# The last block's column halves copied out of PSUM by one VectorE instruction each, in place of a VectorE and a ScalarE copy

## Chip, cores, metric

The kernel runs on one core of one Trainium2 chip. The metric is device time of one execution in microseconds (us), lower is better. The kernel before takes 317.51 us (median of 3 runs, 317.42 to 317.64). Runs that agree are expected to lie within a few tenths of a per cent; a verdict of "faster" or "slower" is given only beyond 2%. A run is said to be fast when it is not over 1.5% above the fastest run of its kernel.

## The reference

Linear attention over 8 batches and 8 heads, then a gated feed-forward block. Cut to what matters:

```python
q_s = softmax(q, axis=-1);  k_s = softmax(k, axis=2)        # 8 x 8 x 576 x 64
kv  = einsum('bhsd,bhse->bhde', k_s, v)
x   = einsum('bhsd,bhde->bhse', q_s, kv)   # -> 4608 tokens x 512
g   = x @ w_gate;  val = x @ w_val         # 512 -> 1536
out = (silu(g) * val) @ w_out              # 1536 -> 512, float32
```

The change touches the last 128 tokens of the last product, the out-projection. Its matmuls write to a memory called PSUM, which is divided into banks; the result is copied from there to a second memory, SBUF (this copy is also called the evacuation), and the stores to the output read SBUF. A store is issued by an engine on its queue, and has landed when the semaphore that tells of its completion is updated.

## The kernel before

The out-projection is done in 36 blocks of 128 tokens. An ordinary block is 12 matmuls of 512 columns into one PSUM bank, one copy to SBUF, and two stores of 64 rows each, both on the sync queue:

```python
def o_out(j, o_ps, eng=nc.vector):
    o_sb = osb.tile([128, 512], FP32, tag="o_sb", name="o_sb")
    copy(eng, o_sb, o_ps)
    store(j, o_sb)                      # two stores, both on the sync queue
```

The last block is different, since nothing follows that could hide its copy and its stores. It is made in two column halves of 256, so that the first half is copied and stored while the second is multiplied, and each half's copy is shared between two engines:

```python
def o_last(j):
    r0 = (j * 128) % RING
    o_sb = osb.tile([128, 512], FP32, tag="o_sb", name="o_sb")
    for c0 in (0, 256):
        o_ps = bank("o_ps")                       # one PSUM bank per half
        for m in range(MT):                       # 12 matmuls of 256 columns
            nc.tensor.matmul(
                out=o_ps[:, 0:256], lhsT=hr[:, m, r0:r0 + 128], rhs=wo[:, m, c0:c0 + 256],
                start=(m == 0), stop=(m == MT - 1),
            )
        nc.vector.tensor_copy(out=o_sb[:, c0:c0 + 128], in_=o_ps[:, 0:128])
        nc.scalar.copy(out=o_sb[:, c0 + 128:c0 + 256], in_=o_ps[:, 128:256])
        store(j, o_sb, c0, c0 + 256, (nc.sync, nc.scalar))   # rows 0-63 sync, 64-127 scalar queue
```

A tile framework puts in the semaphores between engines.

The softmax here doesn't subtract the row's maximum and nothing guards it: scores larger than these inputs give would overflow.

## Time and profile before

| | before |
|---|---|
| time, median of 3 | 317.51 us |
| span of the profiled run | 316.0 us |
| matmul engine busy | 304.7 us, 96% |
| last matmul's end to the last stores' issue | 0.65 us |
| last stores' issue to landing (sync, scalar queue) | 1.93, 2.19 us |
| last matmul's end to the end of the span | 4.04 us |

(The last three rows are differences of time stamps in the trace.)

The page of the kernel before, its line of the span, its busy line and the head of the chain that ended last. PE is the matmul engine, DVE is VectorE, ACT is ScalarE:

```profile
span 316.0 us, 4856 instructions
PE 304.7 (96%) x1865; PEld 152.0 (48%) x1894; DVE 163.2 (52%) x277; ACT 147.6 (47%) x218; POOL 28.0 (9%) x35
PE 88%; DMA 4%; DVE 3%; ACT 2%; issue 1%; POOL 1%; SPq 0%; DVEq 0%
```

The kernel is bound by matmuls almost from end to end. The change can only act where no matmul hides anything, which is after the last one. The chain of waits there, of the kernel before (start, duration, what):

```profile
309.31 2.63 PE o_ps L342 x24
311.95 0.02 issue
311.97 0.30 DVE o_sb L346
312.27 0.02 issue
312.30 0.27 ACT o_sb L347
```

The same stretch in the timeline of the kernel before (start, duration, engine, line, operation; the bracket holds the engine's idle time before it and what ended it; SPq and ACTq are the issues of stores on the sync and the scalar queue):

```profile
311.97 0.29 DVE L346 COPY o_sb<-o_ps 128x128 f32<-128x128 f32 x1 [1.02 <-PE o_ps L342]
312.30 0.27 ACT L347 COPY o_sb<-o_ps 128x128 f32<-128x128 f32 x1 [1.04 <-DVE o_sb L346]
312.59 0.47 SPq L316 DMA_DIRECT2D out_dram<-o_sb  x1
312.59 0.50 ACTq L316 DMA_DIRECT2D out_dram<-o_sb  x1
```

The matmuls end at 311.94. ScalarE has been idle for a microsecond, and yet it starts its copy only when VectorE's ends. The view of waits of the last microseconds of the kernel before names it as well:

```profile
ACT o_sb L347 <- DVE o_sb L346: 1.0, 1, 1.0
DVE o_sb L346 <- PE o_ps L342: 1.0, 1, 1.0
```

So the sharing makes two copies in a row, not two at once. What VectorE copies from PSUM cost at several widths, from the groups of instructions by shape of the kernel before (count | busy us, mean ns | idle before):

```profile
L113 DVE COPY o_sb<-o_ps 128x512 f32<-128x512 f32 x33 | 22.4, 680 | 39.2 <-PE o_ps L322 37.3 <-remote 1.9
L113 DVE CAST xt<-xp 128x256 bf16<-128x256 f32 x5 | 2.0, 417 | 0.0
L346 DVE COPY o_sb<-o_ps 128x128 f32<-128x128 f32 x2 | 0.6, 292 | 1.6 <-PE o_ps L342 1.6
```

The mean of 680 ns for 512 columns mixes slightly different records; the copies of the last blocks, read one by one, take 691 to 692 ns.

### The profile page before, as it was taken

Reading aid. Unit: us, or ns where it says so; the run is one execution under the profiler, and the core shown is the slowest. Engines: PE = TensorE matmul, PEld = TensorE weight load, DVE = VectorE, ACT = ScalarE, POOL = GpSimd, SP = SyncE. Lnnn points to the kernel's source line nnn. Section 1 sums busy time; section 2 is a strip of 40 time slices with the busy share of each in tenths; the row PEclk is TensorE's granted clock in tenths of the full one; section 3 lists DMA queues with packets and bytes.
Section 4 is the critical chain, followed back from the end, with each engine's and each line's share of the span. In section 5 each row is a group of like instructions: output and inputs, shape, how many; then the busy total and the mean of one; then the engine's idle time right before and its main releaser. Section 6 shows DMA issues by size and latency. Waiting matters only on the chain.

```text
span 316.0 us, 4856 instructions
## 1 busy us (share of the span) xinstructions
PE 304.7 (96%) x1865; PEld 152.0 (48%) x1894; DVE 163.2 (52%) x277; ACT 147.6 (47%) x218; POOL 28.0 (9%) x35
## 2 busy tenths in 40 slices
PE   6799999999999999999999999999999999999994
PEld 2477744554444444544454444544454444444443
DVE  3834476685754566455835492639354333423421
ACT  4743488634663465447354637355743113312300
POOL 2930021100200020002000200020000000000000
PEclk9999999999999999999999999999999999999999
DMA  7999999269246806490629253944310202020124
GB/s 269 183 204 207 296 393 391 68 160 364 50 91 179 338 17 128 112 394 11 141 68 352 97 110 66 322 162 103 66 41 0 65 3 66 0 68 3 31 68 102
DMA packets 39304, 45.75 MB, mean 145 GB/s; under 512 B 16368, under 2 KB 23024, under 8 KB 39280
## 3 DMA queue, kind: packets, MB, share of 16 engines
q1 hardware_dynamic: 32480, 39.99, 42.0%
q0 software_dynamic: 6640, 5.31, 10.9%
q8 instruction: 15, 0.25, 0.3%
q10 hardware_dynamic: 160, 0.13, 0.2%
q14 instruction: 9, 0.07, 0.1%
HBM read 37.75 MB, written 9.44 MB: 149 GB/s over the span
## 4 chain that ended last, share of the span: by engine, by line
PE 88%; DMA 4%; DVE 3%; ACT 2%; issue 1%; POOL 1%; SPq 0%; DVEq 0%
PE g_ps L298 29%; PE u_ps L298 29%; PE o_ps L322 25%; PE kv L191 3%; DMA wv<-in_moe_w_val_dram 2%; DMA k<-in_k_dram 2%; DVE rs L138 1%; PE xp L267 1%; DVE qs L152 1%; PE o_ps L342 1%; ACT L124 1%; ACT eq L124 1%; POOL v L361 0%; PE tp L166 0%; POOL v L358 0%
## 5 line engine op out<-in xcount | busy, mean ns | idle before, releaser
L305 ACT ACTIVATE sg<-g_ps 128x512 bf16<-128x512 f32 (+2 forms) x120 | 65.1, 554 | 139.1 <-PE g_ps L298 120.7
L306 DVE TENSOR_TENSOR hr<-sg,u_ps 128x512 bf16<-128x512 bf16 (+2 forms) x120 | 74.5, 630 | 87.8 <-PE u_ps L298 80.4
L298 PE MATMUL g_ps<-xt,wg 128*128 128x512 bf16 (+2 forms) x469 | 110.0, 358 | 1.0 <-ACT xt L111 0.2
L298 PE MATMUL u_ps<-xt,wv 128*128 128x512 bf16 (+2 forms) x468 | 109.8, 357 | 1.2 <-DMA wv<-in_moe_w_val_dram 0.5
L322 PE MATMUL o_ps<-wo,hr 128*128 128x512 bf16 x414 | 93.0, 379 | 0.4 <-issue 0.2
L298 PEld LDWEIGHTS <-wv 128*128 128x128 bf16 x480 | 46.9, 98 | 47.2 <-DMA wv<-in_moe_w_val_dram 0.9
L298 PEld LDWEIGHTS <-wg 128*128 128x128 bf16 x480 | 45.8, 98 | 45.3 <-issue 0.7
L322 PEld LDWEIGHTS <-hr 128*128 128x128 bf16 x420 | 40.9, 98 | 49.1
L113 DVE COPY o_sb<-o_ps 128x512 f32<-128x512 f32 x33 | 22.4, 680 | 39.2 <-PE o_ps L322 37.3
L127 POOL CAST vb<-v 128x1152 bf16<-128x1152 f32 x14 | 16.0, 1146 | 174.3 <-DMA v<-in_v_dram 111.8
L138 DVE TENSOR_REDUCE rs<-eq 128x18 f32<-128x1152 bf16 (+2 forms) x18 | 21.7, 1214 | 13.2 <-ACT eq L124 13.2
L152 DVE TENSOR_TENSOR qs<-eq,rr 128x1152 bf16<-128x1152 bf16 (+2 forms) x18 | 22.1, 1237 | 0.1
L124 ACT ACTIVATE eq<-q 128x1152 bf16<-128x1152 f32 (+2 forms) x18 | 18.1, 1050 | 4.5 <-DMA q<-in_q_dram 4.4
L124 ACT ACTIVATE ek<-k 128x1152 bf16<-128x1152 f32 x16 | 18.0, 1158 | 0.3 <-DMA k<-in_k_dram 0.2
L305 ACT ACT_TABLE_LOAD x12 | 15.4, 1283 | 0.2
L124 ACT ACT_TABLE_LOAD x11 | 14.1, 1283 | 0.2
L388 PE MATMUL idle<-zero 128*128 128x512 bf16 x20 | 6.1, 459 | 3.0 <-DVE rs L138 1.8
L191 PE MATMUL kv<-vb,ek 64*128 64x129 bf16 x252 | 8.7, 217 | 0.0
L191 PEld LDWEIGHTS <-ek 64*128 64x128 bf16 x252 | 7.3, 94 | 2.7 <-ACT sg L305 2.1
L275 ACT CAST xt<-xp 128x512 bf16<-128x512 f32 x12 | 6.4, 588 | 3.6 <-PE xp L267 3.6
L276 DVE CAST xt<-xp 128x512 bf16<-128x512 f32 x12 | 7.7, 683 | 0.0
L347 ACT COPY o_sb<-o_ps 128x128 f32<-128x128 f32 x2 | 0.5, 265 | 13.3 <-DVE o_sb L346 13.3
(46 smaller groups left out, 70.2 us busy)
## 6 DMA issues: line engine op xcount, KB each, us to landing
q<-in_q_dram SPq DMA_DIRECT2D x16, 576.0 KB, 5.6
k<-in_k_dram SPq DMA_DIRECT2D x16, 576.0 KB, 7.3
out_dram<-o_sb SPq DMA_DIRECT2D x70, 128.0 KB, 2.3
v<-in_v_dram SPq DMA_DIRECT2D x14, 576.0 KB, 9.0
wo<-in_moe_w_out_dram POOLq DMA_DIRECT2D x4, 384.0 KB, 16.3
wg<-in_moe_w_gate_dram POOLq DMA_DIRECT2D x2, 384.0 KB, 9.7
wv<-in_moe_w_val_dram POOLq DMA_DIRECT2D x2, 384.0 KB, 10.7
wg<-in_moe_w_gate_dram POOLq DMA_DIRECT2D x1, 512.0 KB, 13.7
```

What stands on the lines that cost most here:

```text
L113: eng.tensor_copy(out=out, in_=in_)
L124: nc.scalar.activation(out=e[:, t0:t1], in_=src[:, t0:t1], func=AF.Exp)
L127: nc.gpsimd.tensor_copy(out=vbs[G][:, :, 0:128].rearrange("p t (h d) -> p t h d", d=64), in_=raw["v", b, G].rearrange("p h (t d) -> p t h ...
L138: i = nc.vector.reduce_sum(out=rs[:, 2 * t0:2 * t1], in_=eq2[:, 2 * t0:2 * t1, :], axis=mybir.AxisListType.X)
L152: eng.tensor_mul(qs[:, t0:t1, :].rearrange("p t (h d) -> p (t h) d", d=64), eq2[:, 2 * t0:2 * t1, :], s["rr"][:, 2 * t0:2 * t1].to_broadca ...
L191: nc.tensor.matmul(out=kv[g][:, c:c + 129], lhsT=ek_of(b, G, g, t), rhs=vbs[G][r, t, 0:129], start=(t == 0), stop=(t == T - 1),)
L275: nc.scalar.copy(out=xt[:, 2 * G, c0:c0 + 512], in_=main[G][0])
L276: nc.vector.tensor_copy(out=xt[:, 2 * G + 1, c0:c0 + 512], in_=main[G][1])
L298: nc.tensor.matmul(out=gu[a][i][:, 0:w_], lhsT=(wg, wv)[a][:, kk, ms], rhs=xt[:, kk, c:c + w_], start=(kk == 0), stop=(kk == KT - 1),)
L305: nc.scalar.activation(out=sg[:, 0:w_], in_=g_ps[:, 0:w_], func=AF.Silu)
L306: nc.vector.tensor_mul(hr[:, m, r:r + w_], sg[:, 0:w_], u_ps[:, 0:w_])
L322: nc.tensor.matmul(out=o_ps, lhsT=hr[:, m, r0:r0 + 128], rhs=wo[:, m, :], start=(m == 0), stop=(m == MT - 1),)
```

## The change

The intent is to pay one copy's fixed cost and no hand-over between engines, in place of two fixed costs and a hand-over.

```diff
-            nc.vector.tensor_copy(out=o_sb[:, c0:c0 + 128], in_=o_ps[:, 0:128])
-            nc.scalar.copy(out=o_sb[:, c0 + 128:c0 + 256], in_=o_ps[:, 128:256])
+            nc.vector.tensor_copy(out=o_sb[:, c0:c0 + 256], in_=o_ps[:, 0:256])
             store(j, o_sb, c0, c0 + 256, (nc.sync, nc.scalar))
```

## The prediction

> **What bounds the kernel now.** The page of the profile before (span 316.0 us) has the matmul engine busy 96% of the span at a granted clock of 0.998; the chain of waits is 88% matmul. The change touches none of that, only the tail after the last matmul, where everything is exposed. The timeline of the last microseconds: last matmul of the second column half ends at 311.94 (chain of waits); VectorE copy 128x128 starts 311.97, takes 0.29; ScalarE copy 128x128 starts 312.30, takes 0.27; both store issues (sync and scalar queues) start at 312.59, take 0.5, land 1.9 and 2.2 us later; then closing waits, to 316.0. So the two copies do not run side by side: the view of waits says the ScalarE copy waited for the VectorE copy, though their columns are disjoint, and the built program has that wait. Both read one PSUM bank; the Trainium skill, "PSUM — Partial Sum Buffer", Terms, says no two engines may access the same bank at once. The trace agrees: 312.30 is after 312.26. No overlap is lost by giving up ScalarE.
>
> **What it removes and adds.** Per half it removes a ScalarE copy (265 ns) and one hand-over between engines (some 35 ns from end to start), and makes the VectorE copy 256 columns wide. VectorE took 692 ns for 128x512 f32 from PSUM and 292 ns for 128x128: 1.04 ns a column and about 159 ns fixed. An estimate from these for 128x256 is 425 ns (casts of 128x256 from PSUM took 417). The Trainium skill, "VectorE: DVE Perf Modes", errata section, gives 120 + columns cycles at 0.96 GHz for PSUM to SBUF, 392 ns for 256; the trace is 33 ns above that at both measured sizes, which again gives 425. Stores keep queues, sizes and order; in the built program they wait for VectorE in place of ScalarE. Everything earlier is unchanged.
>
> **On the critical path.** Matmul end to store issue is 0.65 us before (0.03 + 0.29 + 0.04 + 0.27 + 0.02). After: 0.03 + 0.425 + 0.02 = 0.47. Saved: 0.17 to 0.18 us, once. The first half gains the same, but its copies and stores lie under the second half's matmuls, so that is worth nothing.
>
> **Predicted time:** 317.51 - 0.17 = 317.34 us, 0.05% less. The spread of the three runs before (317.42 to 317.64) is larger than the gain, so medians may stand in either order; 8 times in 10 between 317.10 and 317.62. Chances: faster by over 2% 0.002, within 2% 0.996, slower by over 2% 0.002.
>
> **What would show each step right or wrong.** Right: one VectorE copy of 128x256 per half, 0.41 to 0.44 us; no ScalarE copy of the output block in the tail; both last stores issued 0.45 to 0.49 us after the last matmul; issue to landing (1.9 to 2.4 us) and landing to end unchanged; span near 315.8. Wrong: a copy over 0.55 us; stores that wait longer after the copy's end than now (0.02 us), above all on the scalar queue, which now waits for another engine instead of its own copy; a longer landing that gives the 0.17 us back.
>
> **What would make it wrong.** A copy cost not linear between the measured widths; a slower start of the scalar queue's store when that engine has been idle; landing times, which vary by 0.5 us among the last stores, hiding the gain in single runs.

## The result, and the profile after

The changed kernel takes 317.37 us (median of 6 runs, 317.25 to 318.02); the kernel before, in the same rounds and the earlier ones, 317.47 us (6 runs, 317.37 to 318.08). The ratio is 0.9998 with a 95% interval of 0.9985 to 1.0011. (Ratios here are the mean time of one kernel's fast runs over that of the other's of the same rounds, so they are not quite the ratios of the medians quoted.) At this resolution not even the sign is known: the interval is some 0.8 us wide, the expected gain is 0.17 us. What the change does has to be read from the trace.

The page of the kernel after, the same lines:

```profile
span 316.2 us, 4851 instructions
PE 306.3 (97%) x1865; PEld 152.5 (48%) x1894; DVE 163.3 (52%) x277; ACT 147.1 (47%) x216; POOL 28.1 (9%) x35
```

ScalarE has two instructions fewer and VectorE as many as before. The span of this run is 0.2 us longer, not shorter; it is the slowest of the six (318.02 us). Its chain of waits at the end:

```profile
309.48 2.63 PE o_ps L342 x24
312.11 0.02 issue
312.14 0.42 DVE o_sb L346
```

Its timeline after the last matmul:

```profile
312.14 0.42 DVE L346 COPY o_sb<-o_ps 128x256 f32<-128x256 f32 x1 [0.89 <-PE o_ps L342]
312.59 0.47 SPq L316 DMA_DIRECT2D out_dram<-o_sb  x1
312.60 0.50 ACTq L316 DMA_DIRECT2D out_dram<-o_sb  x1
```

And its line on the two copies, with their shortest, median and longest duration in ns:

```profile
L346 DVE COPY o_sb<-o_ps x2: 423/424/425, 310.8 to 312.1; 128x256 f32<-128x256 f32 x2
```

Three things are to be seen. The copy of 256 columns takes 424 ns, as predicted (425). From the last matmul's end to the issue of the last stores it is now 0.49 us, where it was 0.65: 0.16 us saved, as predicted within 0.02. And the last matmul itself ends 0.16 us later than in the profile before (312.10 against 311.94), although nothing before it was changed. Over the profiles of kernels that do the same work up to there (before, after, and the repeats below), this end lies between 311.46 and 312.11. That scatter of 0.65 us is four times the saving, and it is large enough to hide it in the medians.

There is one loose end. The stores of this profile land later after their issue than those of the profile before. The line on the landing of the last two stores (shortest, median, longest), first of before, then of after:

```profile
DMA to landing us min/median/max: 1.9/2.1/2.2
```

```profile
DMA to landing us min/median/max: 2.2/2.3/2.4
```

With the later landing, the time from the last matmul's end to the end of the span is 4.11 us after, against 4.04 before. If that is caused by the change, the saving is given back; if it is scatter, it is not. This was the first thing to test.

### The profile page after: what moved, and what is told of

Its sections match the earlier page's. It is cut to its first block, busy times and chain, and to the rows that moved or that the text cites. A ratio compares the mean times of both kernels' runs of the same rounds, so it can differ in the third digit from the quotient of the medians.

```text
span 316.2 us, 4851 instructions
## 1 busy us (share of the span) xinstructions
PE 306.3 (97%) x1865; PEld 152.5 (48%) x1894; DVE 163.3 (52%) x277; ACT 147.1 (47%) x216; POOL 28.1 (9%) x35
## 4 chain that ended last, share of the span: by engine, by line
PE 88%; DMA 4%; DVE 3%; ACT 2%; issue 1%; POOL 1%; SPq 0%; DVEq 0%
PE g_ps L298 29%; PE u_ps L298 29%; PE o_ps L322 25%; PE kv L191 3%; DMA wv<-in_moe_w_val_dram 2%; DMA k<-in_k_dram 2%; DVE rs L138 1%; PE xp L267 1%; DVE qs L152 1%; PE o_ps L342 1%; ACT L124 1%; ACT eq L124 1%; POOL v L360 0%; PE tp L166 0%; POOL v L357 0%
## 5 line engine op out<-in xcount | busy, mean ns | idle before, releaser
L387 PE MATMUL idle<-zero 128*128 128x512 bf16 x20 | 7.8, 555 | 2.7 <-DVE rs L138 1.5
L113 DVE CAST xt<-xp 128x128 bf16<-128x128 f32 (+2 forms) x14 | 4.9, 374 | 2.8 <-PE xp L220 2.8
```

What stands on the lines that cost most here:

```text
L113: eng.tensor_copy(out=out, in_=in_)
L387: i = nc.tensor.matmul(out=idle, lhsT=zero[:, 0:128], rhs=zero, start=True, stop=True)
```

## The experiments

Twelve kernels ran, all correct. The names used for theories are those of the expectations: A is that the saving is real, is the difference of one and two instructions in a row, and is kept; B is that slower landing gives it back.

### The changed kernel twice more, and the kernel before once more

No edit.

> The changed kernel once more, unaltered. Theory A (the saving of about 0.18 us before the last store issue is kept): last matmul to store issue 0.45 to 0.49 us again, issue to landing scattered between 1.9 and 2.4 us as before, time 0.1 to 0.25 us under the kernel before where the rounds can resolve it. Rival B (the saving is given back: landing became slower because of the change): both last stores land 2.2 to 2.4 us after issue again, 0.2 us more than the 1.9 and 2.2 of before, and the times are equal within 0.1 us.

> The kernel before once more, unaltered, for a second profile of it. Theory A: last matmul to store issue 0.64 to 0.66 us; issue to landing anywhere in 1.9 to 2.4 us, so that it may exceed that of the changed kernel. Rival B (landing is slower in the changed kernel because of the change): 1.9 and 2.2 us again. Time ratio 1.000 within 0.002.

> The changed kernel a third time. Last matmul to store issue 0.45 to 0.50 us; the scalar store lands 2.18 to 2.45 us after issue (2.40 and 2.21 in its two traces, 2.19 and 2.18 in those of before); if the saving is kept on the whole, last matmul to the end of the span is 3.87 to 3.95 us in most traces against 4.04 in both of before; if landing is slower because of the change, it is 4.05 or more again.

Measured, from the traces (us; the first row of each kernel is the profile shown above):

| profile | last matmul's end | to store issue | scalar store, issue to landing | sync store, issue to landing | last matmul's end to end of span |
|---|---|---|---|---|---|
| before | 311.94 | 0.65 | 2.19 | 1.93 | 4.04 |
| before, again | 311.46 | 0.65 | 2.18 | 1.92 | 4.04 |
| after | 312.10 | 0.49 | 2.40 | 2.21 | 4.11 |
| after, again | 312.11 | 0.49 | 2.21 | 1.92 | 3.91 |
| after, third | 311.67 | 0.49 | 2.20 | 1.92 | 3.89 |

The landing line of the third profile of after:

```profile
DMA to landing us min/median/max: 1.9/2.1/2.2
```

The longer landing did not come back, so B falls as a steady effect; that a late landing now and then is likelier after the change, three profiles against two cannot exclude. In two of three profiles the tail is 0.13 to 0.15 us shorter than before; the first profile had a landing 0.2 us late. In that profile the last data packets of the last stores ended 2.34 us after the last matmul, as in the other two (2.34 and 2.35) and earlier than before (2.50 and 2.49), so as far as the packet records go it was mainly the notice of completion that came late. Why it did is open.

The times again resolve nothing. After, again: 317.65 us against 317.56, ratio 0.9997 (0.9985 to 1.0010). After, third: 317.42 against 317.52, ratio 1.0005 (0.9991 to 1.0018). Before, again: 317.57 against 317.70, ratio 0.9995 (0.9980 to 1.0010); that is the kernel before compared with itself, and its ratio lies as far from 1 as the changed kernel's.

Pooled, the changed kernel has a mean of 317.53 us (16 runs, standard error 0.09) and the kernel before 317.58 us (35 runs, standard error 0.04): a difference of 0.05 with an error of 0.10, which fits nothing saved, and is also only a little over one error away from 0.17 us saved.

### The saving magnified 25 times

A gain too small for the clock can be repeated until it is large. In these kernels the second half's matmuls are done into two banks with the same values, and the evacuation is made 25 times over. The three differ only in who copies, and from which bank:

```diff
+            if c0 == 256:
+                o_p2 = bank("o_ps")
             for m in range(MT):
-                nc.tensor.matmul(out=o_ps[:, 0:256], ...)
+                for o in (o_p2, o_ps) if c0 == 256 else (o_ps,):
+                    nc.tensor.matmul(out=o[:, 0:256], ...)
+            for _ in range(25 if c0 == 256 else 1):
# many_one:
+                nc.vector.tensor_copy(out=o_sb[:, c0:c0 + 256], in_=o_ps[:, 0:256])
# many_split:
+                nc.vector.tensor_copy(out=o_sb[:, c0:c0 + 128], in_=o_ps[:, 0:128])
+                nc.scalar.copy(out=o_sb[:, c0 + 128:c0 + 256], in_=o_ps[:, 128:256])
# many_split_banks: as many_split, but
+                nc.scalar.copy(..., in_=(o_p2 if c0 else o_ps)[:, 128:256])
```

> The saving magnified. In the last half the matmuls are done into two banks (12 more of 256 columns, some 1.3 us), and the evacuation is made 25 times over (the same values): here one VectorE copy of 256 columns each time. Theory A: each repeat costs the 0.424 us of one copy plus 0.0 to 0.06 us of waiting for itself, 24 repeats add 10.2 to 11.6 us; total 328.8 to 330.3.

> As many_one, but each of the 25 evacuations is the pair of before, 128 columns on VectorE, then 128 on ScalarE, from one bank. Theory A (serial, two fixed costs and two hand-overs): 0.29 + 0.04 + 0.265 + 0.04 = 0.63 us a pair, 24 repeats add 15.1 us, total about 333.7, 3.5 to 5 us more than many_one (0.17 to 0.2 us each). A rival in which the pair's cost in the tail was a chance of one trace: no difference from many_one, or a shorter time.

> As many_split, same copies and sizes, same output tile, but ScalarE reads the second bank, with the same values. Theory A (only the shared bank makes the pair serial): the two engines run side by side, 0.29 to 0.36 us a pair, 24 repeats add 7 to 8.6 us, total 325.5 to 327.5, clearly under many_one. Rival E (the shared output tile, or the hand-over between the engines, makes the pair serial): still some 0.63 us a pair, total as many_split, about 333.7.

| | time (median of 4) | against before (317.70) | per evacuation, against one VectorE copy |
|---|---|---|---|
| one VectorE copy | 329.52 us | 1.0370 | |
| pair, one bank | 333.84 us | 1.0507 | +0.17 us (4.32 / 25) |
| pair, two banks | 326.29 us | 1.0269 | -0.13 us (-3.23 / 25) |

All three lie where theory A put them. The timelines, each of a stretch within the repeats; first one VectorE copy at a time (five copies in 2.26 us; a new one starts every 0.46 us, which is 0.424 of copy and 0.035 of waiting for itself):

```profile
315.62 2.26 DVE L350 COPY o_sb<-o_ps 128x256 f32<-128x256 f32 x5
```

The pair from one bank, where the engines take turns, a pair every 0.63 us:

```profile
315.72 0.29 DVE L350 COPY o_sb<-o_ps 128x128 f32<-128x128 f32 x1 [0.33 <-ACT o_sb L351]
316.05 0.27 ACT L351 COPY o_sb<-o_ps 128x128 f32<-128x128 f32 x1 [0.36 <-DVE o_sb L350]
316.34 0.29 DVE L350 COPY o_sb<-o_ps 128x128 f32<-128x128 f32 x1 [0.33 <-ACT o_sb L351]
```

The pair from two banks, where they run side by side, six in 1.92 us:

```profile
315.74 1.92 DVE L350 COPY o_sb<-o_ps 128x128 f32<-128x128 f32 x6
315.99 1.76 ACT L351 COPY o_sb<-o_ps 128x128 f32<-128x128 f32 x6
```

Two things follow. The 0.17 us per evacuation is shown on the clock, not only in the trace, and it passes in full into the time: the traces have 4.16 us between the ends of the last copies of the two, counted from the last matmul, and the times differ by 4.32. The tail hides nothing of it. And the reason why the split is slower is the shared bank: same engines, same sizes, same output tile, another bank, and the pair is the fastest of the three. Rival E falls. The two-bank form is no better kernel as it stands, for it computes the half twice; filling two banks without that means 24 matmuls of 128 columns in place of 12 of 256, which no run here tried.

### ScalarE alone for the last half

If the number of instructions in a row is what counts, the engine does not have to be VectorE.

```diff
-            nc.vector.tensor_copy(out=o_sb[:, c0:c0 + 256], in_=o_ps[:, 0:256])
+            if c0 == 0:
+                nc.vector.tensor_copy(out=o_sb[:, c0:c0 + 256], in_=o_ps[:, 0:256])
+            else:
+                nc.scalar.copy(out=o_sb[:, c0:c0 + 256], in_=o_ps[:, 0:256])
```

> The last half copied by ScalarE alone, 256 columns in one instruction, the first half by VectorE alone. ScalarE casts of 128x256 from PSUM took 378 ns in the trace before, VectorE copies 424 ns in the trace after. Theory A: what counts is one instruction in place of two, so last matmul to store issue is about 0.42 us, 0.05 us shorter than after, and the total is not to be told from that of after (0.05 us). Rival C (VectorE as such was the point, ScalarE reads PSUM or hands over slower): the copy takes over 0.5 us and the store issue comes later than in after.

> As many_one, but the 25 evacuations of the last half are by ScalarE alone, 256 columns each. Theory A (count of instructions and their own time are all that matters): 0.37 us as in act_last plus 0.03 us of waiting for itself, 0.40 us each against 0.46, so 24 x 0.06 = 1.4 us less than many_one's 329.5: 327.8 to 328.4. Rival C (VectorE as such is the better engine for this copy): the same as many_one or more.

Once in the tail: 317.28 us (5 runs) against 317.56 for before, ratio 0.9992 (0.9980 to 1.0005). The trace of it, after the last matmul (which ended at 311.54):

```profile
311.58 0.37 ACT L349 COPY o_sb<-o_ps 128x256 f32<-128x256 f32 x1 [13.25 <-PE o_ps L342]
311.98 0.47 SPq L316 DMA_DIRECT2D out_dram<-o_sb  x1
311.98 0.51 ACTq L316 DMA_DIRECT2D out_dram<-o_sb  x1
```

Store issue is 0.43 us after the last matmul, 0.06 less than in after; the last matmul's end to the end of the span is 3.87 us. Repeated 25 times it takes 328.21 us, 1.31 us less than VectorE alone (329.52; the two ran in different calls, with before at 317.52 and 317.70, so of the 0.05 us per copy some 0.01 is uncertain). The group of the 25 copies in that trace:

```profile
L353 ACT COPY o_sb<-o_ps 128x256 f32<-128x256 f32 x25 | 9.3, 372 | 15.3 <-DMA out_dram<-o_sb 14.6
```

Rival C, that VectorE is the better engine here, falls: ScalarE's copy of 256 columns is 52 ns shorter (372 against 424). The gain of the change comes from "one instruction in place of two", not from VectorE.

### The last block not split at all

```diff
-        for c0 in (0, 256): ...      # the whole body of o_last
+        o_unit(j)                    # 12 matmuls of 512, one copy of 512, two stores on the sync queue
```

> The last block not split by columns: 12 matmuls of 512 columns, one VectorE copy of 128x512, two 128 KB stores on the sync queue. If the tail adds up serially, the copy takes 0.69 us in place of 0.42 (0.27 us more), the second store is issued about 0.5 us after the first as both are on one queue, the matmuls take about the same (2.59 against 2.63 us): 0.7 to 0.9 us longer than after, about 318.1 to 318.3. Were the tail hidden behind something else, the time would stay at that of after.

Measured 318.87 us (4 runs), ratio to before 1.0048 (1.0027 to 1.0070). The direction was right and the size too small by about a third: the expectation was 0.7 to 0.9 us over after, the medians of the same rounds differ by 1.2 us (318.87 against 317.65). The trace has last matmul to the end at 5.11 us, 1.0 to 1.2 more than the three profiles of after. The copy is 0.69 us and the first store is issued at 0.76 us after the last matmul, as expected. The second store, on the same queue, is issued not 0.5 but 0.83 us after the first, at 1.59, and each lands 2.3 us after its issue. Between the end of the one issue and the start of the other lie 0.36 us, for which the view of waits names nothing; in the ordinary block just before it only 0.04 us lie between the two. This pause matters in the next experiment.

### Making the first half late

The prediction gave the gain on the first half no value. To see how far that half is off the critical path, its copy is made twice or three times:

```diff
-            nc.vector.tensor_copy(out=o_sb[:, c0:c0 + 256], in_=o_ps[:, 0:256])
+            for _ in range(3 if c0 == 0 else 1):      # first_thrice; 2 in first_twice
+                nc.vector.tensor_copy(out=o_sb[:, c0:c0 + 256], in_=o_ps[:, 0:256])
```

> As after, but the copy of the first half is made three times (the same values), 0.85 us or more of added VectorE work; the trace of after shows VectorE idle for 0.89 us between the two copies. Theory A says that the first half's copy is off the critical path: copy of the last half still starts within 0.1 us of the last matmul, last matmul to store issue within 0.1 us of 0.47, total within 0.15 us of after. Rival D (the first half's copy and its stores count too, through the queues): its stores go out some 0.9 us later, and the last stores are issued or land 0.3 to 0.9 us later.

> A smaller dose of first_thrice: the first half's copy made twice, its stores are ready 0.46 us later than in after (about 0.36 us before the last matmul's end). Theory Q, from the traces so far: what delayed the last stores in first_thrice was the store queues, not VectorE[...]. So here: last copy 0.04 to 0.46 us after the last matmul, as in after; the sync queue's first-half issue ends at about 0.2, its last store is issued at 0.62 to 0.68 us in place of 0.49; the scalar queue's last store at 0.48 to 0.52. Total within 0.2 us of after. Rival V (VectorE's added work delays the last copy): the copy ends later than 0.5 us and both stores move together.

first_thrice took 318.21 us (4 runs), ratio 1.0023 (1.0008 to 1.0039), 0.56 us over after in the same rounds. This was a miss for theory A as I had put it, and rival D was right. But the reason is not VectorE. The chain of first_thrice ends with the copies (the last line holds the third copy of the first half and the copy of the last half, each 0.42 us, partly overlapping in the records):

```profile
311.03 0.44 DVE o_sb L347
311.47 0.02 issue
311.49 0.82 DVE o_sb L347 x2
```

It ends at 312.31, 0.46 us after the last matmul (311.85), just as in after. Then the stores of first_thrice, of which the last pair starts 0.75 and 1.02 us after the last matmul, where in after it is 0.49:

```profile
312.60 0.72 ACTq L316 DMA_DIRECT2D out_dram<-o_sb  x1
312.86 0.47 SPq L316 DMA_DIRECT2D out_dram<-o_sb  x1
```

The first half's stores were issued only at 0.10 us after the last matmul and held both queues until 0.56 (sync) and 0.66 (scalar). On each queue the last store was issued only after that, on the sync queue with a further 0.38 us until its next semaphore step.

That pause is not what follows any store, as I had taken it. In the kept traces the steps that follow a store issue on the sync queue without a wait come 0.04 to 0.06 us after it, over 50 times in each. The pause of 0.36 to 0.38 us comes once in a trace, always ahead of the 208th instruction that the profile records on the sync engine: in before and after (0.363 and 0.378 us) as in first_thrice and first_twice (0.377), and in whole (0.364), where that instruction is a store and not a semaphore step. (In act_last_freed, below, that instruction waits for its copy in any case, and the pause is not seen.) So it belongs to a place in the program. What happens there is open. In before and after it ends before the last copy does and costs nothing; in first_thrice it makes some 0.33 us of the 0.53 us by which the last sync store is late (an estimate: 0.38 less the usual 0.05).

The smaller dose, first_twice, tests the reading that the queues, and not VectorE, make the last stores late. The first half's stores are issued at -0.36 and leave the sync queue at 0.10 and the scalar queue at 0.20. Its last copy and stores (last matmul's end at 311.66):

```profile
311.69 0.42 DVE L347 COPY o_sb<-o_ps 128x256 f32<-128x256 f32 x1 [0.43 <-PE o_ps L342]
312.15 0.52 ACTq L316 DMA_DIRECT2D out_dram<-o_sb  x1
312.22 0.47 SPq L316 DMA_DIRECT2D out_dram<-o_sb  x1
```

The copy ends where it does in after, the scalar queue is in time at 0.49, and the sync queue alone is late, at 0.56 (I had expected 0.62 to 0.68, as I had put the end of its earlier issue at 0.2). The time is 317.50 us, ratio 1.0007 (0.9991 to 1.0022), the tail 3.89 us, as in after: the sync store, now issued second, lands last, at 2.73 us after the last matmul, where in the third profile of after the scalar store was last at 2.70. So the first half has slack, but a limited one: 0.14 us on the sync queue at after's timing (its first-half issue ends at -0.11, plus the pause of 0.38 and 0.08 to the issue gives 0.35; the last store is issued at 0.49) and none at all when that issue is late. In the second profile of after it ended at +0.06 and the sync queue's last store came at 0.50, 0.01 after the scalar queue's.

### A version meant to beat both

ScalarE alone for the last half, and the second store of the block before it on the scalar queue, to free the sync queue earlier:

```diff
-        store(j, o_sb)
+        store(j, o_sb, engs=(nc.sync, nc.scalar if j == n_tok // 128 - 2 else nc.sync))
```

with the edit of act_last above.

> act_last, and the second store of the block before the last moved to the scalar queue, so that the sync queue's first-half store goes out earlier. Theory Q: the sync queue is ready for its last store some 0.15 us earlier, which buys nothing as long as the copy ends later than that: last stores issued 0.42 to 0.45 us after the last matmul as in act_last, total within 0.1 us of act_last and 0.1 to 0.3 us under before, too little to be a verdict of its own.

The sync queue is done with its first-half store at -0.35 us in place of -0.11, the last stores are issued 0.43 us after the last matmul, as in act_last, and the last matmul's end to the end of the span is 3.85 us, the shortest of all profiles (before 4.04, after 3.89 to 4.11, act_last 3.87). The time is 317.41 us (5 runs, 316.82 to 317.76) against 317.52, ratio 0.9996 (0.9984 to 1.0009). By the trace it is 0.19 us better than before; by the clock it is not told apart. Pooled, the two kernels with ScalarE alone at the end have a mean of 317.34 us (10 runs, standard error 0.09), 0.25 us under the kernel before with an error of 0.10: a sign in the expected direction, from runs on several chips, and no proof. That the freed queue bought nothing beyond act_last was expected.

## Why the prediction was right

- "The two copies do not run side by side", because of the bank: right. The program's wait and the trace said so before; the two-bank experiment shows it by 0.30 us a pair (333.84 - 326.29, divided by 25). The Trainium skill, "PSUM — Partial Sum Buffer", Terms, says that no two engines may access one bank within a partition at once. (The prediction left out "within a partition"; both copies cover all 128 partitions, so it makes no difference here.) This agrees so far as the program keeps the engines apart and never breaks the rule; what an overlap would do was not tried.
- The copy at 425 ns: measured 424. Two widths from the trace before, and a straight line between, were enough. The Trainium skill, "VectorE: DVE Perf Modes", errata section, gives 120 + columns cycles at 0.96 GHz for PSUM to SBUF, as estimates 258, 392 and 658 ns for 128, 256 and 512 columns; the traces have 292, 424 and 692, so 32 to 34 ns more at each.
- 0.17 to 0.18 us saved between the last matmul and the store issue: 0.16 measured in three profiles. The missing 0.01 is rounding of small terms: from the last matmul to the copy it is 0.037 us (taken as 0.03) and from the copy to the issue 0.028 (taken as 0.02), both nearly as before (0.037 and 0.025).
- Landing and everything after it unchanged: right in two profiles of three; in the first, which fell on the slowest run, landing took 0.2 us more. The range for the total (317.10 to 317.62) rested on such scatter and held 317.37.
- "Span near 315.8" was not met by the first profile (316.2), but by scatter of the last matmul's end and of the landing; the others have 316.0 and 315.6.
- The first half's gain "is worth nothing": right for the change, as the tail shortened only by what the last half saved. The reason given, that its copies and stores lie under the second half's matmuls, was too simple: they also hold the queues that the last stores need, and in first_thrice a delay of 0.9 us there costs 0.56 us, the pause on the sync queue included.
- The predicted total itself, 317.34, is confirmed only in the sense that nothing contradicts it. That it lies 0.03 us from the measured median is luck: the six runs spread over 0.8 us. That 0.17 us is what a split evacuation costs was shown on the clock by repetition; that the total fell by it was not resolved.

## What to carry to other kernels

Before two engines share one copy out of PSUM, look whether both read the same bank: if they do, they took turns in every trace here, and one instruction on one engine (for 256 columns rather ScalarE than VectorE) is shorter than both halves. A change of a tenth of a microsecond in a tail is below what the total time can show; read it between two time stamps of the trace, take more than one profile, and repeat the disputed piece in a test kernel until the clock shows it. When work in a tail is made shorter, look at what stands in order ahead of the last stores on their queues, for that is the next limit.

## What the Trainium skill lacked or had wrong

- "VectorE: DVE Perf Modes", errata section: the PSUM to SBUF rule for VectorE, 120 + columns cycles, gives 32 to 34 ns less than the durations that the profile shows at 128, 256 and 512 columns (292, 424, 692 ns). The same table's ScalarE rule, 172 + columns cycles at 1.2 GHz, gives as estimates 250 and 357 ns for 128 and 256; measured 266 and 372. By the two rules ScalarE would be the shorter by 35 ns at 256 columns of float32; measured it is by 52 ns.
- "DMA: Bandwidth & Descriptors", the table of where the fixed 2 us of a DMA go, has most of them as the receipt of the write, after the last byte. It stands in the section on DMAs issued from GpSimd, so it does not speak of these stores, which the sync and scalar queues issue, and the page has no such table for them. In the kernel before the last stores divide their time otherwise: issued at 312.59, their first packets run about 1.1 us later, and their last packet ends 0.35 us before the later of the two landings. Shown here by the DMA view of the kernel before, 40 slices of 0.075 us from 312.6 on (the second group of digits is the last pair of stores, 313.7 to 314.4; landings are 1.9 and 2.2 us after the issue). The end of a packet is as the profile records it, and might itself contain some of the receipt.

```profile
DMA  8889887000000005888999410000000000000000
```

- No page that I found has, with a number, the pause of 0.36 to 0.38 us that the sync queue makes once in a trace ahead of its 208th recorded instruction (0.363 in before, 0.378 in after, 0.364 in whole, 0.377 in first_thrice and first_twice; other steps after a store issue come 0.04 to 0.06 us after it). In act_last_freed, with one instruction fewer ahead, that instruction is the last store itself, which waited for its copy in any case, so nothing of the pause is seen. Its cause is open.
